# Attention and feed-forward block in one kernel: tile 1's load moved to SyncE's queue, tile 3's load behind a weight block, one transpose moved behind a pair's no-op

## Chip, cores and metric

One core of a Trainium2 chip. The metric is device time in microseconds (us); lower is better. Engines are named as in the profile: PE (TensorE, matmuls), DVE (VectorE), ACT (ScalarE), POOL (GpSimd), SP (SyncE, which here issues DMAs and carries no-ops).

## The reference

Two branches over the same normalized input are multiplied and added to the input. 2048 tokens, width 448, 16 heads of 28, feed-forward width 1792, bf16.

```
xn = layernorm(x)
q, k, v = split(xn @ wqkv)                 # 448 -> 3*448, 16 heads of 28
# each token attends to 8 tokens: itself and back in steps of 2
o = softmax(q . k[pos - 2*w] / sqrt(28), w = 0..7) . v
s = o @ wo                                 # 448 -> 448
g = silu(gelu(xn @ w1 + b1) @ w2 + b2)     # 448 -> 1792 -> 448
out = x + s * g
```

## The kernel before

The tokens are sorted into even and odd positions, so that the dilated window is a window of neighbours. They are cut into 16 token tiles of 128 rows and four chunks of four tiles. The stages are:

- **Normalization** of a token tile: statistics (line 354, BATCH_NORM_STATS2), their aggregate (358), root and reciprocal (366, 369), and the scaled tile `xn` (391 for tile 0, 422 for the others). The transposed form `xnT` of chunk 0 is made by PE transposes (404, 437) and copies (250, 252); from tile 4 on by a DMA transpose (301).
- **Projections** `qk_rows` (513) and `vproj` (536). The input width of 448 is three row tiles of 128 and a rest of 64, so the weights `w_in` are three loads, one for each row tile (`load_w`), and two tail loads.
- **Feed-forward** `ff1` (589) and its gelu (593), then `ff2_pair` and `ff2` (615, 641).
- **Attention** for nine blocks of tokens: `keys` (700, 698), `scores` (715), the exponentials (721), `values_sum` (746), the division (757, 762). Each block's rows go to a DRAM tile `o_rows` (769). `turn(t)` brings the rows of tiles t and t + 1 back transposed by one DMA transpose (301).
- **Output**: `final_pair` (780) and `final` (795) multiply by `wo`; `store` (803 to 815) gates, adds the input and writes out.

Every instruction group is a task of a plan. A table, ORDER, lists all tasks in the order in which they are emitted; the letter is the engine (P, V, A, G, S for PE, DVE, ACT, POOL, SP; D marks a DMA's landing, and emits nothing) and the number is the task. Each engine executes its own tasks in that order and waits by semaphores. A task's engine may be chosen by the letter where the task allows several.

Two things matter for this change. First, `pair` computes two jobs together on the two halves of PE's rows: a first half (f1), then a no-op on another engine that waits for the first half's last matmuls, then a second half (f3) that waits for the no-op:

```
def f2(k):
    held["told"] = {"POOL": nc.gpsimd, "SP": nc.sync, "ACT": nc.scalar}[k.on].nop()
    for i in held["last"]:
        behind(held["told"], i)
```

The engine of the no-op is the letter in ORDER. All that stands behind the no-op on that engine waits with it. Second, ahead of the first data PE runs idle matmuls on constants (line 265), ten of 512 columns and one of 128. The loads of the start are made by `load_x(t0, n, eng)` (tokens) and `load_w` (weights), all at line 288. The first matmuls on row tiles of tiles 0 and 1 are `first_batch`, in the order row tile 0, row tile 2, row tile 1, with three matmuls (q, k, v) for a token tile.

Of the kernel before, what the change touches and what calls it, by code (L numbers as in the profile page):

```python
# [11 lines left out]
ACT = mybir.ActivationFunctionType  # L12
# [2 lines left out]


ORDER = """
D0 A31 D32 G14 S29 D30 V12 P1 V13 V15 V19 V20 A48 V21 S33 D34 V22 V16 G45 V17 V18 P2 V23 G46 D47 S39 D40 P3 S35 D36
G95 P4 S37 D38 S41 D42 P5 S43 D44 P6 G97 P7 V55 P8 V56 S71 D72 V59 A57 P9 S73 D74 P10 G652 G24 S75 D76 G25 G28 G26 G27
S77 D78 V58 V99 P11 V60 P102 V100 A61 P103 V105 A106 A101 P128 V62 V109 V110 P111 P112 P132 P104 V113 A114 A107 D115  # L20
D108 P129 S81 D82 V63 P184 P133 V64 V67 A65 S83 D84 P130 V66 V116 P131 V117 V68 V185 P118 V98 A69 P119 V96 V120 D121
S85 D86 P134 V70 V122 P149 V123 A135 V136 A139 P124 G150 P125 A146 P151 A49 S137 D138 V126 D127 G147 D148 V142 P296
G140 D141 V152 P301 V153 G297 V91 S154 D155 P163 G302 V89 P298 V90 G164 V92 V87 G94 G264 G265 D266 P303 A300 V143 P165
V79 A305 S144 D145 P316 V194 A166 V198 A299 V195 G167 D168 P311 V199 S196 D197 V80 V88 V169 G317 G93 A304 P318 S200
D201 P306 A319 G312 V186 G170 D171 V187 V190 A320 G172 D173 P313 V191 S188 D189 G307 G174 D175 P156 V653 A314 G176
D177 V654 P308 A315 S192 D193 G157 G178 D179 P158 A310 P291 V159 A160 S256 D257 S258 D259 A309 P321 G292 S262 D263
G180 D181 S260 D261 P293 G322 G182 D183 P225 A294 P323 A295 G226 P227 A325 P267 P485 V229 A324 V273 S161 D162 P505
A228 G486 V275 V277 V279 P487 G506 V274 P495 A488 V276 V268 A489 P507 G496 V278 V280 P497 V282 A509 P475 V284 V286
A508 V283 V285 A498 P209 V288 G476 G210 V287 G281 A499 P477 V289 P216 V334 G217 G290 A478 V335 V338 S336 D337 P211
A479 V339 V330 P480 V213 S340 D341 V212 P218 V326 G481 P490 A219 V327 V331 S214 D215 A222 G220 D221 P482 G491 G223  # L30
D224 V683 P492 A484 S332 D333 V684 P500 A493 V412 A483 P202 V413 S328 D329 G501 A494 V400 P502 G203 V401 S402 D403
P204 A504 P655 V205 P580 A503 V206 S207 D208 S414 D415 A50 G248 D249 G250 D251 A656 P239 A658 A581 V657 V659 V408 V409
S410 D411 P582 G240 S230 D231 P660 V586 P685 A661 P241 V583 V404 V405 S406 D407 A663 P232 V245 V662 A686 P365 V713
V664 A688 G233 V714 A587 P234 A366 V687 V689 A242 P690 G923 V236 P367 A235 V588 P589 A691 S237 D238 G243 D244 A693
V692 V694 G246 D247 A584 S924 D925 A369 V585 S926 D927 A368 P715 S370 D371 G590 P695 P665 V696 A716 P591 V666 V697
A718 V667 V698 V668 V699 V669 G700 D701 P349 V592 G670 D671 S672 D673 P720 V595 A593 G350 P674 G702 D703 P351 V675
A721 G252 D253 V676 P416 A352 A353 G254 D255 A723 P342 G417 V677 S354 D355 V678 A596 P418 G343 V743 G679 D680 P704
V717 A420 P344 G681 D682 V705 A419 V706 P598 A346 S421 D422 V719 V707 A345 A744 V708 G709 D710 S347 D348 V597 G711
D712 P725 V722 G599 P745 V726 P750 V727 A746 P600 S928 D929 A748 V728 V729 A751 V724 G730 D731 S732 D733 A753 V594
V747 V749 P734 V604 P379 V735 A605 V736 P372 G380 V737 P381 V738 G373 P356 V601 G741 S739 D740 D742 A385 S930 D931  # L40
V773 A602 P755 G386 D387 P374 V756 G357 P358 A382 A375 V757 G383 D384 P430 A359 V774 A362 A376 P446 G360 D361 V758
V759 G363 D364 P775 S447 S760 D761 P448 G431 G762 D763 G388 D389 G392 D393 A776 V752 S377 D378 P780 A778 V449 P432
A781 V754 P423 S424 V803 A783 P764 V777 A450 P425 V765 A433 V766 P453 G390 D391 A436 V767 V768 P607 A427 A426 A804
A454 S769 D770 G394 D395 V779 G396 D397 G398 D399 V606 G434 D435 V603 G437 D438 P455 V782 G608 P439 V784 G771 D772
G271 D272 G269 D270 A459 V456 P805 G460 D461 V833 A440 P441 A806 G457 D458 P785 A808 P609 V786 A443 A442 A834 V787
V788 V789 G463 D464 G465 D466 S792 S428 D429 G790 D791 D793 V807 V809 S444 D445 G462 P810 V613 P540 A811 V610 A813
A541 P794 P815 V812 A51 G467 D468 P515 V795 V796 G469 D470 P542 V797 A516 V798 A611 P517 V816 G801 S799 D800 D802 V817
A544 P530 V818 A543 V819 P535 V814 A518 A531 G820 D821 V612 G822 D823 P824 A614 P532 A536 G471 D472 A519 V825 P537
V826 G473 D474 A534 P510 V827 V828 A539 V615 V863 P525 G829 D830 S831 D832 A533 A511 A538 P512 S526 A864 P520 P955
S521 S451 D452 A514 P527 G956 A513 P957 A528 P522 V958 A529 P944 V962 G959 A524 V963 P835 P840 A523 G945 S960 D961  # L50
P946 S964 D965 A52 P616 V947 V951 V952 A841 S953 D954 A843 V842 V948 A836 P865 V844 S949 D950 S934 D935 S932 D933 S936
D937 G617 P870 A838 V837 P618 A871 V839 A873 G872 A866 A868 V867 G874 A893 P845 V622 P625 G869 V846 V847 A623 V848
A894 V849 V619 G850 D851 V624 P854 G852 D853 A620 S626 P895 P627 V855 A896 V856 A898 V857 V858 V621 G859 D860 V897
G861 D862 V899 P550 V631 V628 P966 A632 G551 A629 V633 P900 G967 P977 A901 V630 A903 P968 V902 G978 A53 V904 P545 S938
D939 V973 P979 V974 G546 V969 S975 D976 P552 V980 G970 P905 A554 P547 V906 V907 S971 D972 A553 P555 V908 V981 A549
V909 S982 D983 P875 G556 P557 A548 V984 S910 D911 P884 S912 D913 V876 A559 P575 V877 A558 V885 P570 V886 S576 V887
V888 P577 S571 V878 G889 D890 P572 V879 A578 G891 D892 V985 P999 A579 G880 D881 S986 D987 P560 A574 G1000 G882 D883
A573 P1001 S561 P914 V1002 P562 V915 P565 V916 A563 V1003 A564 P988 V917 S566 S1004 D1005 V918 P567 S940 D941 V1006
G989 G921 P990 V1007 A568 P634 S1008 D1009 V995 A569 S919 D920 D922 V991 A54 V996 P635 V992 S997 D998 S993 D994 P638
V636 A637 S942 D943 P1015 P639 P1010 V640 P642 A641 V1011 V1012 V1016 S1013 D1014 P643 G1017 P646 S1018 D1019 V644  # L60
A645 P647 P1025 A648 P1020 V1026 V1027 P649 V1021 S1028 D1029 P650 P1030 V1022 A651 V1031 S1023 D1024 V1032 S1033
D1034
"""


# [58 lines left out]
def kernel(  # L124
# [13 lines left out]
    P = 128  # L138
# [17 lines left out]
    for v in range(9):  # L156
        n = NW - 1 if v == 4 else NW
# [10 lines left out]
    def rows(halves, pos, n):  # L168
        h, r = divmod(pos, HALF)
        return halves[h, r:r + n, :]  # L170
# [74 lines left out]
    def buf(pool, owner, i=0):  # L245
        return pool.bufs[owner.slots[pool][i]]
# [12 lines left out]

    t_on = plan.add("DMA", lambda _: None, ())  # L260
    t_warm = t_on
    for n in (512,) * 10 + (P,):
        def idle(k, n=n):
            one = nc.const_aps
            nc.tensor.matmul(buf(p_b, k)[:, :n], one.tensor(1.0, [P, P], BF16), one.tensor(1.0, [P, n], BF16), start=True, stop=True)
        t_warm = plan.add("PE", idle, [t_warm], take=(p_b,))
        t_warm.give = ((p_b, t_warm, 0),)
# [18 lines left out]
    def dma(eng, dst, src, deps=()):  # L286
        def fn(_):
            {"SP": nc.sync, "ACT": nc.scalar, "POOL": nc.gpsimd}[eng].dma_start(dst, src)  # L288
        a = plan.add(eng, fn, [t_on] + list(deps))
        return plan.add("DMA", lambda _: None, [a])  # L290
# [35 lines left out]
    load_w(2)  # L326
    tails = A_wqkv[KF:D, :].rearrange("p (w d) -> p w d", d=D)
# [649 lines left out]
```

## Time and profile before

| | |
|---|---|
| three runs | 148.98, 149.68, 151.68 us (median 149.68) |
| the profiled execution's own time | 149.42 us |
| its span, first to last instruction | 147.7 us |
| PE busy | 143.2 us (97%), 1827 matmuls |
| DVE, ACT, POOL busy | 104.7, 95.3, 56.7 us |
| HBM read and written | 9.70 and 6.29 MB |

Busy times are of one profiled execution; its time less its span, 149.42 - 147.7 = 1.7 us, lies outside the first and last instruction. Lines of the timeline give the start in us from the span's start, the duration, engine and line, what is written and read, the shape and the count, and in brackets the idle time ahead with what ended it. "SPq" is the issue of a DMA by SP, not its transfer. The ends of matmuls are modelled, their starts are recorded. Rows by stretches give busy time and count of PE, weight loads, DVE, ACT and POOL, then the granted clock, the share of the 16 DMA engines and GB/s.

### The profile page before, as it was taken

Reading aid. Unit: us, or ns where it says so; the run is one execution under the profiler, and the core shown is the slowest. Engines: PE = TensorE matmul, PEld = TensorE weight load, DVE = VectorE, ACT = ScalarE, POOL = GpSimd, SP = SyncE. Lnnn points to the kernel's source line nnn. Section 1 sums busy time; section 2 is a strip of 40 time slices with the busy share of each in tenths; the row PEclk is TensorE's granted clock in tenths of the full one; section 3 lists DMA queues with packets and bytes.
Section 4 is the critical chain, followed back from the end, with each engine's and each line's share of the span. In section 5 each row is a group of like instructions: output and inputs, shape, how many; then the busy total and the mean of one; then the engine's idle time right before and its main releaser. Section 6 shows DMA issues by size and latency. Waiting matters only on the chain.

```text
span 147.7 us, 4656 instructions
## 1 busy us (share of the span) xinstructions
PE 143.2 (97%) x1827; PEld 79.8 (54%) x1827; DVE 104.7 (71%) x290; ACT 95.3 (65%) x175; POOL 56.7 (38%) x113
## 2 busy tenths in 40 slices
PE   7999999999999999999999999999999999999991
PEld 2345555455566666666665554445565564545570
DVE  3879934179953798979969599728589996671642
ACT  4327576766684682785696889999983886571120
POOL 6743595105430031651476795512463024110200
PEclk9999999999999999999999999999999999999999
DMA  4999999999699799898499979993774332265112
GB/s 146 328 293 336 137 208 153 267 348 244 145 181 152 133 148 203 144 226 143 121 180 168 215 195 119 201 212 100 103 139 113 71 104 64 72 176 126 35 31 62
DMA packets 43966, 24.17 MB, mean 164 GB/s; under 512 B 33822, under 2 KB 42022, under 8 KB 43944
## 3 DMA queue, kind: packets, MB, share of 16 engines
q1 hardware_dynamic: 41080, 17.25, 62.4%
q0 software_dynamic: 2720, 6.51, 18.5%
q8 instruction: 14, 0.23, 0.7%
q10 hardware_dynamic: 144, 0.11, 0.3%
q14 instruction: 8, 0.07, 0.2%
HBM read 9.70 MB, written 6.29 MB: 108 GB/s over the span
## 4 chain that ended last, share of the span: by engine, by line
PE 90%; DMA 4%; DVE 1%; SPq 1%; issue 0%; DVEq 0%
PE bank L589 29%; PE bank L615 22%; PE bank L513 14%; PE bank L641 7%; PE bank L536 7%; PE bank L780 5%; DMA w_in<-in_A_wqkv_dram 4%; PE bank L746 3%; PE bank L715 3%; PE bank L795 1%; SPq L288 1%; DVE sg L803 1%; DVE o L811 0%; PE bank L437 0%; PE bank L898 0%
## 5 line engine op out<-in xcount | busy, mean ns | idle before, releaser
L589 PE MATMUL bank<-xnT,w 64*128 64x512 bf16 x392 | 46.6, 376 | 0.1
L593 ACT ACTIVATE h<-bank,b 128x512 bf16<-128x512 f32 x56 | 35.1, 685 | 13.4 <-PE bank L589 12.9
L615 PE MATMUL bank<-w,h 64*128 64x448 bf16 x336 | 33.8, 349 | 0.0
L589 PEld LDWEIGHTS <-w 64*128 64x128 bf16 x392 | 20.3, 94 | 19.1 <-issue 0.7
L513 PE MATMUL bank<-w_in,xnT 64*128 64x448 bf16 (+1 forms) x212 | 26.4, 350 | 0.2
L615 PEld LDWEIGHTS <-h 64*128 64x128 bf16 x336 | 17.3, 94 | 12.8
L762 DVE TENSOR_TENSOR a<-bank,rd 114x448 bf16<-114x448 f32 (+1 forms) x36 | 22.2, 622 | 1.1
L769 POOL DMA_DIRECT2D o_rows<-a x25 | 13.4, 538 | 24.8 <-DVE a L762 11.2
L721 ACT ACTIVATE E<-bank 128x456 bf16<-128x456 f32 (+1 forms) x36 | 17.4, 551 | 7.0 <-PE bank L715 5.9
L295 POOL DMA_DIRECT2D v<-v_rows x22 | 13.8, 633 | 9.9 <-PE bank L589 7.2
L513 PEld LDWEIGHTS <-xnT 64*128 64x128 bf16 (+1 forms) x212 | 11.2, 94 | 8.2 <-issue 0.6
L657 DVE TENSOR_TENSOR y<-bank,b 128x448 f32<-128x448 f32 x15 | 9.0, 621 | 8.2 <-PE bank L641 4.8
L295 POOL DMA_DIRECT2D v_rows<-v_tok x16 | 9.0, 566 | 14.3 <-PE bank L715 8.6
L536 PE MATMUL bank<-w_in,xnT 64*128 64x448 bf16 (+1 forms) x106 | 13.8, 349 | 0.0
L354 DVE BATCH_NORM_STATS2 st<-x_sb 128x6 f32<-128x448 bf16 x16 | 9.2, 609 | 4.5 <-DMA x_sb<-in_A_x_dram 4.5
L731 DVE TENSOR_TENSOR E<-E,m_gen 128x456 bf16<-128x456 bf16 (+1 forms) x29 | 10.8, 392 | 1.4 <-ACT E L721 1.3
L669 ACT ACTIVATE t<-y 128x448 f32<-128x448 f32 x12 | 6.9, 580 | 7.3 <-DVE y L657 7.3
L641 PE MATMUL bank<-w,h 128*128 128x448 bf16 (+2 forms) x70 | 11.4, 316 | 0.0
L700 DVE TENSOR_SCALAR kb<-qkT,plane 128x512 bf16<-128x512 bf16 x24 | 7.5, 358 | 3.5 <-DMA qkT<-qk_tok 2.1
L811 POOL TENSOR_TENSOR o<-x_sb,sg 128x448 bf16<-128x448 bf16 x3 | 3.1, 1031 | 16.7 <-DVE sg L803 8.7
L250 ACT CAST v_tok<-bank 128x448 bf16<-128x448 f32 x13 | 6.6, 534 | 4.3 <-issue 1.5
L757 DVE RECIPROCAL rd<-bank 114x8 f32<-114x8 f32 (+1 forms) x36 | 7.1, 199 | 2.6 <-PE bank L746 2.4
(86 smaller groups left out, 177.4 us busy)
## 6 DMA issues: line engine op xcount, KB each, us to landing
v_rows<-v_tok POOLq DMA_DIRECT2D x16, 128.0 KB, 3.9
v<-v_rows POOLq DMA_DIRECT2D x14, 128.0 KB, 4.7
out_dram<-o SPq DMA_DIRECT2D x15, 112.0 KB, 1.7
w<-in_B_w_dram SPq DMA_DIRECT2D x2, 784.0 KB
o_rows<-a POOLq DMA_DIRECT2D x23, 64.1 KB, 2.9
w<-in_B_w_dram SPq DMA_DIRECT2D x2, 672.0 KB
x_sb<-in_A_x_dram SPq DMA_DIRECT2D x3, 448.0 KB, 7.3
w_in<-in_A_wqkv_dram SPq DMA_DIRECT2D x3, 336.0 KB, 5.2
```

The costliest lines, as they stand in the source:

```text
L295: nc.gpsimd.dma_start(dst(k), src())
L354: nc.vector.bn_stats(out=buf(p_st, k)[:], in_=x_sb[:, t, :])
L513: return nc.tensor.matmul(ps[:, :D], xnT[r, kt, cs], w, start=start, stop=stop)
L536: return nc.tensor.matmul(ps[:, :D], xnT[r, kt, k0:k0 + P], w, start=start, stop=stop)
L589: return nc.tensor.matmul(ps[:], w1[r, kt, ms], xnT[r, kt, cs], start=start, stop=stop)
L593: nc.scalar.activation(buf(p_h, own, i)[:], buf(p_b, own, i)[:], ACT.Gelu_apprx_tanh, bias=b1[:, mt:mt + 1])
L615: return nc.tensor.matmul(ps[:, :D], buf(*h_at[(c, mt)])[r, j * P:(j + 1) * P], w2[r, mt, :], start=start, stop=stop)
L641: nc.tensor.matmul(ps[:, :n], buf(*h_at[(c, mt)])[:, j * P:(j + 1) * P], w2[:, mt, cs], start=(mt == 0 and not biased), stop=(mt == NMT - 1))
L721: nc.scalar.activation(buf(p_E, k)[:, :n], buf(p_b, a, r)[:, :n], ACT.Exp, scale=SCALE)
L731: (nc.gpsimd if k.on == "POOL" else nc.vector).tensor_tensor(out=E, in0=E, in1=m, op=ALU.mult)
L762: nc.vector.tensor_tensor(out=o, in0=sums(k, e)[:, :, :, :DH], in1=buf(p_rd, rd)[rows].unsqueeze(2).unsqueeze(3).to_broadcast((2 * nq, 8, ...
L769: (nc.gpsimd if k.on == "POOL" else nc.sync).dma_start(o_rows[n + i * nq:n + i * nq + nq, :], buf(p_a, own)[i * nq:i * nq + nq, i, :])
```

## The change

The code that makes tasks changes in two places. One idle matmul of 512 columns is left out, and the loads of tokens 1, 2 and 3 are three loads of one tile on SP, where there was one of tile 1 on ACT and one of tiles 2 and 3 on SP:

```diff
-    for n in (512,) * 10 + (P,):
+    for n in (512,) * 9 + (P,):
...
     load_x(0, 1, "SP")
-    load_x(1, 1, "ACT")
+    load_x(1, 1, "SP")
...
     load_w(0)
-    load_x(2, 2, "SP")
+    load_x(2, 1, "SP")
+    load_x(3, 1, "SP")
     load_w(1)
     load_w(2)
```

ORDER is renumbered throughout (lines behind the new load are one higher). Its tasks otherwise stand in their old order on each engine, but for the three places below. PE executes the same matmuls in the same order, less the idle one.

**SP at the start.** `x_sb` is the tokens, `w_in` 128x1344 a row tile of projection weights, `w_in` with 64 rows the tails. Before:

```order
L288 DMA x_sb<-in_A_x_dram 128x448
L288 DMA w_in<-in_A_wqkv_dram 128x1344 x2
L288 DMA x_sb<-in_A_x_dram 128x2x448
L288 DMA w_in<-in_A_wqkv_dram 128x1344
L288 DMA w_in_65<-in_A_wqkv_dram 64x2x448
L288 DMA w_in_65<-in_A_wqkv_dram 64x896
```

With the change:

```order
L288 DMA x_sb<-in_A_x_dram 128x448 x2
L288 DMA w_in<-in_A_wqkv_dram 128x1344 x2
L288 DMA x_sb<-in_A_x_dram 128x448
L288 DMA w_in<-in_A_wqkv_dram 128x1344
L288 DMA x_sb<-in_A_x_dram 128x448
L288 DMA w_in_65<-in_A_wqkv_dram 64x2x448
L288 DMA w_in_65<-in_A_wqkv_dram 64x896
```

Tile 1 is the second issue (before, it was ACT's first instruction). Then come row tiles 0 and 2, tile 2, row tile 1, tile 3 and the tails.

**DVE at the start**, from the statistics of tile 2 on. `st_96` and `st_97` are the statistics of tiles 2 and 3, `b_71` is the first bias, `m_first` and `m_gen` the attention masks. Before:

```order
L354 BN_STATS st_96<-x_sb 128x6
L358 BN_AGGR mv<-st_96 128x2
L354 BN_STATS st_97<-x_sb 128x6
L369 RECIPROCAL rstd<-sd 128x1
L422 TENSOR_SCALAR xn<-x_sb,mv,rstd 128x448
L427 COPY xn<-xn 128x64
L358 BN_AGGR mv<-st_97 128x2
L885 CAST b_71<-bank_155 128x14
L855 COPY m_first<-m_1_90 128x456
L855 COPY m_gen<-m_0_89 128x456
L252 COPY xnT<-bank_157 128x4x128
```

With the change:

```order
L355 BN_STATS st_96<-x_sb 128x6
L359 BN_AGGR mv<-st_96 128x2
L370 RECIPROCAL rstd<-sd 128x1
L423 TENSOR_SCALAR xn<-x_sb,mv,rstd 128x448
L428 COPY xn<-xn 128x64
L886 CAST b_71<-bank_154 128x14
L355 BN_STATS st_97<-x_sb 128x6
L359 BN_AGGR mv<-st_97 128x2
L252 COPY xnT<-bank_156 128x4x128
```

The statistics of tile 3 and their aggregate stand behind tile 2's normalization. The two mask copies are gone from this place; they follow the copy of tile 3's transposed form.

**SP in the middle.** `xnT<-o_rows` is `turn`, of tiles 0 and 1 in the first row and of tiles 2 and 3 in the second; `o_rows<-a` are stores of attention rows, `qkT` transposes of query and key tiles:

```order
 L301 DMA_TRANSPOSE xnT<-o_rows 128x4x256
-L769 DMA o_rows<-a 57x576 x2
+L770 DMA o_rows<-a 57x576 x3
+L301 DMA_TRANSPOSE qkT<-qk_tok_153 128x8x128
+L770 DMA o_rows<-a 57x576
 L301 DMA_TRANSPOSE xnT<-o_rows 128x4x256
-L769 DMA o_rows<-a 57x576
-L301 DMA_TRANSPOSE qkT<-qk_tok_153 128x8x128
-L769 DMA o_rows<-a 57x576
-L769 DMA o_rows<-a 56x576
+L770 DMA o_rows<-a 56x576
```

The transpose of tiles 2 and 3 stands three issues later. Directly ahead of it stands a no-op (not shown among the rows) that was ACT's: that of the pair which computes queries and keys of tile 14. In ORDER the place reads `A440 P441` before, and `S441 S931 D932 P442` with the change, where `S931` is the transpose.

More of the change, by code (lines that the diff above doesn't have):

```diff
@@ L23 @@
[L23 to L32, printed above, removed]
@@ L58 @@
[L58 to L62, printed above, removed]
+D0 G13 S28 D29 S30 D31 V11 P1 V12 V14 V18 V19 A49 V20 S32 D33 V21 V15 G46 V16 V17 P2 V22 G47 D48 S40 D41 P3 S34 D35
@@ L63 @@
+V1007 G990 G922 P991 V1008 A569 P635 S1009 D1010 V996 A570 S920 D921 D923 V992 A55 V997 P636 V993 S998 D999 S994 D995
+P639 V637 A638 S943 D944 P1016 P640 P1011 V641 P643 A642 V1012 V1013 V1017 S1014 D1015 P644 G1018 P647 S1019 D1020
+V645 A646 P648 P1026 A649 P1021 V1027 V1028 P650 V1022 S1029 D1030 P651 P1031 V1023 A652 V1032 S1024 D1025 V1033 S1034
+D1035
 """
```

70 lines of the change are left out of this document (40 added, 30 removed).

## Prediction

> **What bounds the kernel now.** I read the page's busy times first, then its chain, then the busy time by stretches, to see whether one engine sets the time everywhere.
>
> ```profile
> PE 143.2 (97%) x1827; PEld 79.8 (54%) x1827; DVE 104.7 (71%) x290; ACT 95.3 (65%) x175; POOL 56.7 (38%) x113
> PE 90%; DMA 4%; DVE 1%; SPq 1%; issue 0%; DVEq 0%
> core 0: us, PE busy (x) PEld busy (x) DVE busy (x) ACT busy (x) POOL busy (x), PEclk, DMA share, GB/s
> 5.30:10.50 5.20, 4.92 (x32) 2.53 (x32) 3.91 (x17) 2.04 (x7) 3.35 (x15) 1.00 1.05 327
> 40.00:100.00 60.00, 60.00 (x948) 35.73 (x946) 45.45 (x121) 44.91 (x86) 25.63 (x44) 1.00 1.01 170
> 100.00:144.40 44.40, 44.38 (x564) 24.47 (x558) 31.22 (x72) 26.85 (x47) 11.02 (x15) 1.00 0.39 94
> ```
>
> TensorE (PE) is busy for 60.00 of 60.00 us in the middle and 44.38 of 44.40 behind it. So no move there can bring time; it can only open a stall. What could be gained lies ahead of 10.50, where 5.20 us hold 4.92 of PE work, and the DMA part of the chain (4%) belongs there too. A gain of 2%, about 3.0 us, which is also about what a measurement of this kernel can tell from no change, has no room: the idle time of the whole span is 147.7 - 143.2 = 4.5 us, and most of it lies before the first matmul and behind the last.
>
> **The start: loads.** PE's rows, and the piece of the chain that ends there:
>
> ```profile
> 6.46 0.39 PE L437 MATMUL bank<-ident,xn 128*128 128x128 bf16 x4
> 6.99 0.54 PE L513 MATMUL bank<-w_in,xnT 128*128 128x448 bf16 x2
> 8.24 0.54 PE L513 MATMUL bank<-w_in,xnT 128*128 128x448 bf16 x2
> 8.61 0.35 PE L536 MATMUL bank<-w_in,xnT 128*128 128x448 bf16 x1
> 9.05 0.54 PE L513 MATMUL bank<-w_in,xnT 128*128 128x448 bf16 x2
> 2.66 6.35 DMA w_in<-in_A_wqkv_dram
> ```
>
> The batch at 9.05 waits for the third block of projection weights (row tile 1), issued at 2.66 and landed at 9.01. Matmuls of 448 columns start (8.61 - 8.24) / 2 = 0.19 us apart, so PE was ready at 8.61 + 0.19 = 8.80: 0.25 us of wait. The batch at 6.99 is the first one on row tile 2's weights; PE's work ahead of it ended at 6.46 + 0.39 = 6.85 by modelled ends, so 0.14 us more. No releaser is named for that gap; I take it for the load. These 0.39 us are all that better loads can give.
>
> ```profile
> 0.79 0.39 SPq L288 DMA_DIRECT2D x_sb<-in_A_x_dram  x1
> 1.25 0.89 SPq L288 DMA_DIRECT2D w_in<-in_A_wqkv_dram  x2
> 2.18 0.43 SPq L288 DMA_DIRECT2D x_sb<-in_A_x_dram  x1
> 2.66 1.88 SPq L288 DMA_DIRECT2D w_in<-in_A_wqkv_dram  x3
> DMA  5869999999967998999999999999999999999999
> DMA packets 1777, 2.59 MB, mean 316 GB/s; under 512 B 194, under 2 KB 1393, under 8 KB 1777
> 3.43 0.63 DVE L354 BATCH_NORM_STATS2 st<-x_sb 128x6 f32<-128x448 bf16 x1 [1.52 <-DMA x_sb<-in_A_x_dram]
> 4.19 0.59 DVE L354 BATCH_NORM_STATS2 st<-x_sb 128x6 f32<-128x448 bf16 x1
> 7.90 0.63 DVE L354 BATCH_NORM_STATS2 st<-x_sb 128x6 f32<-128x448 bf16 x1 [0.83 <-DMA x_sb<-in_A_x_dram]
> ```
>
> An issue on SP takes (2.66 - 0.79) / 4 = 0.47 us. Token tile 1, so far on ACT's queue, becomes SP's second issue, so both weight blocks are issued 0.47 us later. Is that the cost? The DMA row covers 1.8 to 10 us: the engines are full from about 2.4 on, at 316 GB/s. Then a landing is set by the bytes ahead. Row tile 2 has the same bytes ahead as before (tiles 0 and 1, row tile 0). Row tile 1 has one token tile (112 KB) fewer, since tile 3 moves behind it: 112 KB / 316 GB/s = 0.35 us earlier, of which PE can use the 0.25 it waited. Bounds: -0.39 (both waits go) to +0.47 (the issue decides). The DMA row is nearer to the byte reading; but the engines are not full in its first slices, so I take -0.15.
>
> The Trainium skill, "DMA: Bandwidth & Descriptors", section "Issuing engines are not separate DMA queues", says that SP and ACT each have only a ring on the same 16 engines. By that rule bringing tile 1 over to SP loses no bandwidth, and the whole price is the order; with separate engines per queue the load would cost SP's queue another 0.35 us. No row here separates the two.
>
> Tile 1 itself: tile 0 was issued at 0.79 and in use at 3.43, 2.64 later; tile 1, issued at 1.25, is then there at 3.89, and VectorE (DVE) reads it at 4.19. Hidden, with 0.30 to spare; the ScalarE issue that disappears is paid nowhere, as ACT then only loads a table.
>
> **The start: DVE.**
>
> ```profile
> 9.35 0.40 DVE L422 TENSOR_SCALAR xn<-x_sb,mv,rstd 128x448 bf16<-128x448 bf16 x1
> 10.02 0.27 DVE L855 COPY m_first<-m 128x456 bf16<-128x456 bf16 x1
> 10.61 0.42 DVE L252 COPY xnT<-bank 128x512 bf16<-128x512 bf16 x1
> 12.80 1.68 DVE L252 CAST qk_tok<-bank 128x448 bf16<-128x448 f32 x3
> 14.66 0.94 PE L536 MATMUL bank<-w_in,xnT 64*128 64x448 bf16 x8
> ```
>
> Tile 2's load is halved, so its statistics start about 0.35 before 7.90, and its normalization before 9.35. Tile 3 now lands behind row tile 1, at 8.66 + 0.35 = 9.0 by the same division, and its statistics (0.63) stand on DVE ahead of the copy at 10.61 that PE's next row pair needs. They end near 10.0, with the aggregate at 10.2: some 0.3 us to spare. If tile 3 came 0.5 late, that copy and PE behind it would be late by 0.2. The two mask copies (0.27 each) move behind tile 3, so the casts at 12.80 begin up to 0.54 later; the first ends near 13.9 instead of 13.4, and the first PE batch that takes one of their banks starts at 14.66. No cost; behind it 0.8 us are left.
>
> **The start: one idle matmul less.**
>
> ```profile
> 0.83 4.53 PE L265 MATMUL bank<-const-bfloat16-1.0 128*128 128x512 bf16 x11 [0.83 <-PEq L961]
> 5.28 0.73 PE L404 MATMUL bank<-ident,xn 128*128 128x128 bf16 x3
> PEclk9999999999999999999999999999999999999999
> ```
>
> Eleven idle matmuls (ten of 512 columns, one of 128: 10.25 units) take 4.53 us, 0.44 a unit; warm, 512 columns at the pace above would be 0.22. So PE runs at half pace there, though the granted-clock row prints full speed from its first slice: here the pace of the matmuls has to tell the clock. Dropping one ends them at about 4.9, and the transposes at 5.28 wait for DVE's data anyhow: no work is saved on the path. What it may cost is the clock: PE is idle for some 0.4 us just before pace doubles. If full pace came later, the four batches of three projection matmuls ahead of 9.05 would take 0.19 longer a matmul: 2.3, less the 0.39 of waits they fill, 1.9 us at most. Nothing is the lower end. I take 0, since 4.1 us of idle matmuls remain and the gap is a tenth of them.
>
> The Trainium skill, "TensorE: Matmul & The Clock Gate", Part 1, speaks against this edit: the gate opens after a busy window of about 3.4 us whose phase is free-running, so fewer phases now find a full window inside the idle matmuls. The trace agrees on the two paces, 0.44 and 0.22 us. A window missed whole, 3.4 us at half pace, would cost an estimated 1.7 us by that page; how much idling a window forgives no run here shows.
>
> **The middle: the no-op and the transpose.**
>
> ```profile
> 72.56 1.32 SPq L301 DMA_TRANSPOSE xnT<-o_rows  x1
> 75.51 0.25 SPq L769 DMA_DIRECT2D o_rows<-a  x1
> 79.70 0.24 SPq L769 DMA_DIRECT2D o_rows<-a  x1
> 82.42 0.92 PE L513 MATMUL bank<-w_in,xnT 64*128 64x448 bf16 x8
> 83.45 0.74 PE L513 MATMUL bank<-w_in,xnT 64*128 64x448 bf16 x6
> 86.19 0.32 SPq L769 DMA_DIRECT2D o_rows<-a  x1
> 97.06 0.35 PE L780 MATMUL bank<-wo,xnT 64*128 64x448 bf16 x1
> ```
>
> The pair of tile 14 has its first half at 82.42 and its second at 83.45; between them stands the no-op, now SP's. SP has nothing between 79.94 and 86.19, so the no-op is reached 3.4 us before the first half ends at 83.34, and passes on as ACT's did. Queued behind it: the transpose of tiles 2 and 3 (1.32, until about 84.7), then the row store of 86.19, untouched. Nothing was held up by the transpose at its old place either: SP's next issue, behind another pair's no-op, stands only at 75.51. The result, needed at 97.06, has 12.4 us from its new issue.
>
> ```profile
> 77.50:83.40 5.90, 5.90 (x92) 3.25 (x88) 4.83 (x14) 4.10 (x8) 4.12 (x8) 1.00 1.15 187
> 83.40:86.20 2.80, 2.80 (x56) 1.62 (x50) 2.02 (x7) 2.60 (x6) 2.63 (x5) 1.00 0.59 161
> 96.67 0.35 DVE L700 TENSOR_SCALAR kb<-qkT,plane 128x512 bf16<-128x512 bf16 x1 [1.35 <-DMA qkT<-qk_pair]
> 100.44 0.61 PE L715 MATMUL bank<-qkT,kb 64*128 64x57 bf16 x32
> ```
>
> The transpose's DMA work leaves a full stretch (share 1.15) for one at 0.59, where (1 - 0.59) x 2.80 = 1.15 us of all engines are free. I size it by its issue, 1.32; up to 0.2 us spill over to what follows. The tile that DVE awaits until 96.67 feeds the scores at 100.44, over 3 us later. Cost 0; at worst all 1.32 us go through ACT and DVE, which wait for that tile too, to PE.
>
> **Sum.** -0.15 (loads) + 0 (DVE) + 0 (idle matmul) + 0 (no-op, transpose), against the profiled execution's 149.42 us, its span of 147.7 and 1.7 around it: 149.27, so **149.3 us**. That execution lies 0.26 below the median of the three, 149.68.
>
> **Rivals.**
> - *Loads gain all.* Both weight blocks land before PE asks: 149.42 - 0.39 = 149.0. For it: 0.35 us fewer bytes ahead of row tile 1. Against: row tile 2 has no fewer. Chance 0.13.
> - *Slower: the clock opens late.* Place: 5.3 to 9 us; price up to 1.9: 149.42 + 1.9 = 151.3, half of it 150.4. It decides once the idle time of 4.9 to 5.28 keeps the gate shut. Against: PE idles a little even now and gets its pace. For: the three runs before span 2.7 us, so something already differs between executions. Chance 0.12.
> - *Slower: the middle stalls.* The no-op is reached late, because SP is held by the row store at 79.70, or the moved transpose pushes the tile of 96.67. The first costs PE nothing until that store is 3.4 us late, then one for one; the second 1.32 at most: 150.7. Chance 0.10.
> - *Nothing moves*, since SP's extra issue eats what fewer bytes give: 149.4, not to be told from the forecast, and counted with it.
>
> **How the numbers follow.** The forecast with its neighbour has 0.65: 149.3, its own range 148.6 to 150.2. With the rivals the range is 148.4 to 151.2; the low end allows for the spread of single runs (148.98 to 151.68), the high end takes in most of the late clock and the middle's stall. Faster by over 2% would need more idle time than PE has: 0.03. Slower by over 2% needs 3 us: a store over 6 us late, or the late clock and the stall together, or something unseen: 0.10. Within 2%: 0.87.
>
> **What would show it.** Right: PE's batch at 9.05 starts at 8.8 to 9.05, tile 3's statistics stand on DVE between 9 and 10 us ahead of the 10.61 copy, the second half of tile 14's pair starts within 0.1 us of the first half's end, and PE's busy share from 40 to 144 stays whole. Wrong: projection matmuls 0.38 us apart behind 6 us (clock); row tile 1 landing at 9.3 or later (issue decides); a PE gap near 83.4 (no-op) or 100 (transpose).

## The result, and the profile after

| | before | changed |
|---|---|---|
| median of 21 runs each | 149.67 us (148.64 to 151.68) | 150.12 us (148.93 to 151.85) |
| ratio, 95% interval | 1 | 1.0049 (1.0026 to 1.0072) |
| profiled execution, its span | 149.42, 147.7 us | 150.32, 148.6 us |

The change costs 0.49%. That is within 2%, and the time lies in the predicted range, but the sign is wrong: the forecast was slightly faster, and the interval (1.0026 to 1.0072) excludes a kernel that is as fast as the one before. Ratios here and below compare fast executions alone while medians take in all, so a ratio is not the quotient of two medians, and the profiles of e3 and e9 are of slow executions (151.80 and 152.30 us) and stand outside the table below.

Busy times of the page and two stretches (columns as in the prediction's rows):

```profile
PE 143.1 (96%) x1826; PEld 79.2 (53%) x1826; DVE 105.2 (71%) x290; ACT 95.0 (64%) x175; POOL 56.9 (38%) x113
40.00:100.00 60.00, 60.00 (x948) 35.63 (x944) 45.77 (x124) 44.30 (x85) 26.59 (x46) 1.00 0.97 173
100.00:145.40 45.40, 45.35 (x572) 24.94 (x568) 31.94 (x73) 27.85 (x49) 11.03 (x15) 1.00 0.39 93
```

From 40 us on PE is as full as before. So the 0.9 us of longer span arose earlier. PE's timeline of the changed kernel, from the first transposes to chunk 1's first `ff1` pair:

```profile
4.75 0.64 PE L405 MATMUL bank<-ident,xn 128*128 128x128 bf16 x3
6.18 0.54 PE L514 MATMUL bank<-w_in,xnT 128*128 128x448 bf16 x2
8.00 0.54 PE L514 MATMUL bank<-w_in,xnT 128*128 128x448 bf16 x2
10.04 0.93 PE L514 MATMUL bank<-w_in,xnT 64*128 64x448 bf16 x8
12.46 1.03 PE L590 MATMUL bank<-xnT,w 64*128 64x512 bf16 x7 [0.49 <-DMA w<-in_B_w_dram]
26.07 0.91 PE L514 MATMUL bank<-w_in,xnT 64*128 64x448 bf16 x7 [0.40 <-DVE qk_pair L252]
28.95 2.33 PE L590 MATMUL bank<-xnT,w 64*128 64x512 bf16 x20 [0.46 <-DMA xnT<-xn]
```

and the last of these places before:

```profile
11.09 0.93 PE L513 MATMUL bank<-w_in,xnT 64*128 64x448 bf16 x8
12.94 0.61 PE L589 MATMUL bank<-xnT,w 64*128 64x512 bf16 x4
28.05 2.32 PE L589 MATMUL bank<-xnT,w 64*128 64x512 bf16 x19
```

The start did gain: the row pair of tiles 2 and 3 starts 1.05 us earlier (10.04 for 11.09), the first `ff1` pair still 0.48. About half of that gain is tile 0, which is there 0.58 us earlier now that tile 1's load follows it on SP. DVE's first statistics show it (3.43 before):

```profile
2.85 0.63 DVE L355 BATCH_NORM_STATS2 st<-x_sb 128x6 f32<-128x448 bf16 x1 [0.94 <-DMA x_sb<-in_A_x_dram]
```

They start at 2.84 to 2.94 in all eleven profiles of kernels that load tile 1 from SP, and at 3.33 to 3.51 in the nine that load it from ACT.

Behind the start PE waits three times, as the brackets of its rows show: for w1's first half at 12.46, for a bank that DVE frees at 26.07, for chunk 1's transposed rows at 28.95. At this last place it is 0.90 us late, and this 0.90 arrives at the end of the span (148.6 - 147.7).

What is late shows on SP and DVE. SP's transposes of both kernels, the changed one first:

```profile
11.31 9.29 SPq L301 DMA_TRANSPOSE qkT<-qk_tok  x3
20.70 5.27 SPq L301 DMA_TRANSPOSE xnT<-xn  x4
```

```profile
12.36 7.52 SPq L301 DMA_TRANSPOSE qkT<-qk_tok  x3
19.97 5.16 SPq L301 DMA_TRANSPOSE xnT<-xn  x4
```

The three query/key transposes start 1.05 earlier and are through 0.72 later (20.60 for 19.88). Chunk 1's rows, `xnT<-xn`, stand behind them in SP's queue and are issued by 25.97 instead of 25.13, 0.84 later. DVE of the changed kernel, and the first of these rows before:

```profile
14.34 1.16 DVE L355 BATCH_NORM_STATS2 st<-x_sb 128x6 f32<-128x448 bf16 x2 [0.53 <-DMA x_sb<-in_A_x_dram]
24.30 1.18 DVE L701 TENSOR_SCALAR kb<-qkT,plane 128x512 bf16<-128x512 bf16 x4 [3.12 <-DMA qkT<-qk_tok]
25.41 0.60 DVE L252 CAST qk_pair<-bank 128x448 bf16<-128x448 f32 x1
```

```profile
23.38 1.15 DVE L700 TENSOR_SCALAR kb<-qkT,plane 128x512 bf16<-128x512 bf16 x4 [2.15 <-DMA qkT<-qk_tok]
```

DVE's key copies wait 3.12 us for the third transpose, and the cast that frees PE's bank stands behind them. DVE also waited 0.53 for tiles 4 to 7. So the loads behind the start are late, though no byte was added to them. Two things could make them late. They are issued later, since SP has two loads more ahead of them: w1's first half at 5.51 instead of 4.58, tiles 4 to 7 at 7.32 instead of 6.97. And fewer bytes move at the start. The transfers between 3 and 4 us, changed and before (last column GB/s):

```profile
3.00:4.00 1.00, 1.00 (x4) 0.37 (x3) 0.97 (x3) 0.21 (x1) 0.81 (x4) 1.00 0.81 159
```

```profile
3.00:4.00 1.00, 1.00 (x4) 0.36 (x3) 0.57 (x1) 0.00 (x0) 0.81 (x4) 1.00 1.19 328
```

With tiles 0 and 1 one behind the other on one queue and the first weight block third, half the bytes move in that microsecond. This holds for all profiles: 137 to 237 GB/s in the ten with tile 1 as SP's second issue, 279 to 364 in the nine with it on ACT. Over the first 20 us it is 225 to 241 GB/s against 235 to 254, the same direction with overlap.

**A measure for the rest.** From the row pair (10.04, 11.09) to chunk 1's first `ff1` pair PE has the same work in all kernels. The smallest distance is 16.80 us, and ten profiles have it within 0.01. What lies over 16.80 is waiting (in the changed kernel 2.11 us, of which the three rows above name 1.35). A kernel whose row pair comes late can show 0.00 because its data had more time, so the two columns ahead are to be read with it:

| kernel | row pair | chunk 1 | over 16.80 |
|---|---|---|---|
| before | 11.09 | 28.05 | 0.16 |
| changed; again (e16); third (e18) | 10.04; 10.53; 10.45 | 28.95; 28.45; 29.28 | 2.11; 1.12; 2.03 |
| e1 start alone | 10.35 | 27.85 | 0.70 |
| e12 tile 1 on SP alone | 10.38 | 27.57 | 0.39 |
| e5 w1's second half on ACT | 10.41 | 28.42 | 1.21 |
| e13 three waits opened | 10.55 | 27.58 | 0.23 |
| e2, e4, e6, e8, e10, e14, e15, e17 (tile 1 on ACT) | 10.44 to 11.54 | 27.25 to 28.34 | 0.00 |
| e7 tails on ACT; e11 weights second | 12.69; 11.11 | 29.49; 27.91 | 0.00 |

The profiles of e3 (tile 1 on SP alone, as e12) and e9 would stand at 2.91 and 0.51.

### The profile page after: what moved, and what is told of

Same layout as the page of the kernel before. It is cut to its first block, busy times and chain, and to the rows that moved or that the text cites. A ratio compares the mean times of both kernels' runs of the same rounds, so it can differ in the third digit from the quotient of the medians.

```text
span 148.6 us, 4654 instructions
## 1 busy us (share of the span) xinstructions
PE 143.1 (96%) x1826; PEld 79.2 (53%) x1826; DVE 105.2 (71%) x290; ACT 95.0 (64%) x175; POOL 56.9 (38%) x113
## 4 chain that ended last, share of the span: by engine, by line
PE 77%; DMA 12%; SPq 4%; DVE 3%; issue 1%; DVEq 0%
PE bank L590 22%; PE bank L616 21%; PE bank L514 10%; PE bank L642 7%; PE bank L537 5%; PE bank L781 5%; DMA x_sb<-in_A_x_dram 5%; DMA qkT<-qk_tok 5%; SPq L288 4%; DMA xnT<-xn 3%; PE bank L747 3%; PE bank L716 3%; PE bank L796 1%; DVE st L355 1%; DVE sg L804 1%
## 5 line engine op out<-in xcount | busy, mean ns | idle before, releaser
L590 PE MATMUL bank<-xnT,w 64*128 64x512 bf16 x392 | 47.9, 376 | 0.9 <-DMA w<-in_B_w_dram 0.5
L514 PE MATMUL bank<-w_in,xnT 64*128 64x448 bf16 (+1 forms) x212 | 27.2, 350 | 0.4 <-DVE qk_pair L252 0.4
L537 PE MATMUL bank<-w_in,xnT 64*128 64x448 bf16 (+1 forms) x106 | 14.2, 349 | 0.0
```

Of the source, the lines that this page charges most:

```text
L514: return nc.tensor.matmul(ps[:, :D], xnT[r, kt, cs], w, start=start, stop=stop)
L537: return nc.tensor.matmul(ps[:, :D], xnT[r, kt, k0:k0 + P], w, start=start, stop=stop)
L590: return nc.tensor.matmul(ps[:], w1[r, kt, ms], xnT[r, kt, cs], start=start, stop=stop)
```

## The experiments

All ratios are to the kernel before, on the same chip; each kernel has 12 times, e16 has 6.

### e1, e2: which half of the change

The theory ("A" in the expectations): the loss is chunk 1's rows, turned late. The rivals: the middle, chance, or one edit of the start by itself. e1 is the changed kernel with the middle of before; e2 the kernel before with the middle of the change (its ORDER has the task numbers of the kernel before):

```diff
 e1
-A386 V774 A603 P756
+A386 S931 D932 V774 A603 P756
...
-V834 S441 S931 D932 P442
+V834 A441 P442
 e2
-A385 S930 D931 V773 A602
+A385 V773 A602
...
-V833 A440 P441
+V833 S440 S930 D931 P441
```

> All edits of the start as in the change (token tile 1 on SP's queue, tiles 2 and 3 loaded apart, statistics reordered, one idle matmul less); the middle as before. Theory A (the start's loads put the first query/key transposes ahead of the same loads of w1 and tiles 4 to 7, these transposes then finish later, and tile 4 to 7's normalised rows turn later): the whole loss is here, 1.005 of the time before (about +0.7 us), first transposes near 4.75 us, chunk 1's first ff1 pair near 28.9 us instead of 28.05. Theory E (the no-op and the transposes in the middle cost it): no loss, 0.997 to 1.001. Theory F (the late transposes are chance of one execution): 1.000 on the median.

> Only the middle of the change: the no-op on SP, two output transposes behind it; the start as before. Theory A: 1.000 (within 0.001), since the two profiles stand 0.97 to 0.99 us apart on both sides of the edit. Theory E: 1.005.

Measured: e1 150.05 us, 1.0035 (1.0000 to 1.0070); e2 149.08 us, 0.9988 (0.9960 to 1.0016). The two intervals overlap a little, but e1 has PE wait 0.70 at chunk 1 and e2 nowhere: the loss sits in the start. The rows of e2 show more: its start is that of before, and yet its transposes are through at 18.46, where the profile of before had 19.88.

```profile
10.49 0.93 PE L513 MATMUL bank<-w_in,xnT 64*128 64x448 bf16 x8
11.76 6.70 SPq L301 DMA_TRANSPOSE qkT<-qk_tok  x3
27.29 2.98 PE L589 MATMUL bank<-xnT,w 64*128 64x512 bf16 x26
```

The same steps in the same order ended up to 1.4 us apart between executions. So 0.60 of the 1.05 us that the start seemed to gain was a late execution of before. The four profiles with the start of before have the row pair at 10.49 (e2), 10.54 (e14), 11.09 and 11.54 (e6, where PE waits 0.87 for the second weight block), the seven with the whole new start at 10.04 to 10.55.

### e3, e12, e4: one edit of the start at a time

e3 and e12 are one kernel, before with tile 1 on SP; e4 is before with tiles 2 and 3 apart and DVE's new order:

```diff
 e3, e12
-    load_x(1, 1, "ACT")
+    load_x(1, 1, "SP")
 e4
-    load_x(2, 2, "SP")
+    load_x(2, 1, "SP")
+    load_x(3, 1, "SP")
```

> Only token tile 1's load moved from ACT's queue to SP's, second there. Theory A: tile 0 lands near 2.8 us instead of 3.41 and the first transposes start near 4.8 us; whether the loss comes with it tells whether the earlier first rows alone do the harm: 1.002 to 1.005 if they do. Theory B (the queue that tile 1 takes costs it, because each SP load then stands behind one more): the same 1.005 with w1 and tiles 4 to 7 landing over 0.3 us later than before. If split loads matter instead: 1.000.

> Only tile 1's load on SP's queue, the rest as before: the kernel of e3 again, whose interval (0.997 to 1.004) left open whether this edit alone costs anything. Theory G: 1.002 to 1.005 over both sets of runs. If tile 1's queue only costs together with the split of tiles 2 and 3: 1.000.

> Only tiles 2 and 3 loaded apart (tile 3 behind row tile 1) and the vector engine's order of the start that goes with it; tile 1 on ACT's queue and ten idle matmuls as before. Theory A: row tile 1 lands near 7.6 to 8.0 us, so the first rows gain 0.5 to 1.0 us at 8 us; the qkT transposes go out earlier and the loss is here: 1.003 to 1.005. Theory C (one more DMA and the later copies of masks cost it): the same, but with the gap at the first ff1 batch or at a mask, not at 25 to 29 us. If tile 1's queue is the cause: 1.000.

Measured: e3 149.58 us, 1.0006 (0.9968 to 1.0044); e12 149.68, 1.0002 (0.9964 to 1.0040); e4 149.50, 1.0006 (0.9967 to 1.0045). Neither edit alone has a cost that these runs show; the 1.002 to 1.005 that was expected of e12 isn't met, though its interval doesn't exclude it. The profiles say more about tile 1: e12's has 0.39 us of waits and e4's none, and e3's, of one of that kernel's longest executions, has PE wait 1.00 at 26.81 and 0.81 at 30.05. Both profiles of this kernel have the thin transfers too (184 and 175 GB/s between 3 and 4 us).

### e5, e6: is it SP's own queue?

The first form of theory A said that the transposes stand behind w1's second half in SP's queue. These kernels issue it from ACT, the changed kernel (e5) and the one before (e6):

```diff
+        q = "ACT" if i else "SP"
-        t_w1.append([dma("SP", w1[:, 0:3, cs], ktiles(B_w1[0:KF, cs]))]
-                    + [dma("SP", w1[64 * i:64 * i + 64, 3, cs], B_w1[KF:D, cs]) for i in range(2)])
+        t_w1.append([dma(q, w1[:, 0:3, cs], ktiles(B_w1[0:KF, cs]))]
+                    + [dma(q, w1[64 * h:64 * h + 64, 3, cs], B_w1[KF:D, cs]) for h in range(2)])
```

> The changed kernel with the three loads of w1's second half issued from ACT's queue, behind tile 2's deviation, instead of SP's; the first query/key transposes on SP then stand behind no load of w1's second half in their own queue. Theory A (the lost gain is these transposes behind that backlog): the three transposes are through SP's queue 1 us or more before 20.6 us, the first ff1 pair of chunk 1 starts near 28.1 to 28.5 us instead of 28.95, and the time is 148.7 to 149.6, under the changed kernel's 150.1. Rival (the engines are simply full with bytes, whichever queue they come from): transposes still end near 20 us, 150.0. Rival F (chance): the ratio to the kernel before stays between 1.000 and 1.007.

> The kernel before with the same move of w1's second half to ACT's queue. Theory A: its own transposes end earlier too, but its tensor engine, which starts later, has little left to wait for at 25 to 29 us, so 0.995 to 1.000; the scatter of its runs (148.6 to 151.3) shrinks. Rival (bytes): 1.000.

Measured: e5 149.94 us, 1.0041 (1.0003 to 1.0078); e6 149.55, 1.0003 (0.9971 to 1.0035). e5's issues on ACT and SP's transposes:

```profile
7.70 1.63 ACTq L288 DMA_DIRECT2D w<-in_B_w_dram  x3
11.68 7.96 SPq L301 DMA_TRANSPOSE qkT<-qk_tok  x3
```

The transposes are through at 19.64, for 20.06 to 20.63 in the changed kernel's three profiles (and 19.41 in e1), and the time stays. The test isn't clean, since the edit does two things. SP is held less by the three issues (1.33, 2.39 and 1.45 us, for 1.95, 3.40 and 3.29 in the changed kernel), and PE no longer waits at 26 and 28 us. But w1's second half now moves together with tiles 4 to 7. These, issued at 7.32 in both kernels, are there at 15.69 instead of 14.34; what the third transpose reads comes later by as much, and PE waits at 18.21 and 19.55 instead (0.27 and 0.29). So e5 moves the loss and doesn't settle what SP's queue order is worth. The Trainium skill, "DMA: Bandwidth & Descriptors", section "Issuing engines are not separate DMA queues", says that transfers started by different engines run on the same 16 DMA engines and interleave. The trace agrees (15.69 for 14.34).

### e7, e8, e11: what makes the loads late

e7 issues the two tail loads of the changed kernel from ACT, e8 puts tile 1 back on ACT and leaves all else of the change, e11 issues the first weight block ahead of tile 1:

```diff
 e7
-dma("SP", w_in3[:64], ...), dma("SP", w_in3[64:], ...)
+dma("ACT", w_in3[:64], ...), dma("ACT", w_in3[64:], ...)
 e8
-    load_x(1, 1, "SP")
+    load_x(1, 1, "ACT")
 e11
-D0 G13 S28 D29 S30 D31 V11 P1 V12 V14 V18 V19 A49 V20 S32 D33
+D0 G13 S28 D29 V11 P1 V12 V14 V18 V19 A49 V20 S32 D33 S30 D31
```

> The changed kernel with the two loads of the weights' last rows (the tails of w_in) issued from ACT's queue behind the first deviation, so that SP issues two loads less ahead of w1 and tiles 4 to 7. Theory G (the loss is SP's issue time: each load costs its queue about 0.46 us, and the change puts two more there, so w1 and tiles 4 to 7 land 0.8 us later): tiles 4 to 7 land near 13.4 us instead of 14.3, w1's second half near 16.9 instead of 17.8, and the time falls to 148.9 to 149.6. Theory A without G (only that the transposes are issued earlier): 150.0 as the changed kernel.

> The changed kernel with token tile 1 back on ACT's queue: tiles 2 and 3 apart, one idle matmul less and the middle's no-op stay. Theory G with the hole (with tiles 0 and 1 on one queue the transfers between 3 and 4 us fall from 328 to 159 GB/s, which is never made up): the hole is filled again, 149.2 to 149.7, a ratio to before of 0.997 to 1.001. If the split of tiles 2 and 3 alone does it: 1.003 to 1.005.

> The changed kernel with the first weight load ahead of tile 1's on SP, so that the transfers between 3 and 4 us aren't thin; SP issues as many loads as in the changed kernel. Theory G by bytes (the loads are late because 0.17 MB were not moved at 3 to 4 us): over 280 GB/s there, tiles 4 to 7 land 0.3 to 0.8 us earlier, first ff1 pair 0.3 to 0.6 us later since tile 1 comes later, chunk 1 no later: 149.2 to 149.7. Theory G by issues (each issue on SP's queue counts): tiles 4 to 7 as late as in the changed kernel, and the tile that comes later adds: 150.0 to 150.5.

Measured: e7 149.66 us, 1.0039 (0.9998 to 1.0081); e8 149.14, 0.9973 (0.9939 to 1.0007); e11 150.43, 1.0069 (1.0032 to 1.0106). e8, its transfers between 3 and 4 us and its rows:

```profile
3.00:4.00 1.00, 1.00 (x4) 0.36 (x3) 0.61 (x1) 0.00 (x0) 0.81 (x4) 1.00 1.00 352
10.44 0.93 PE L514 MATMUL bank<-w_in,xnT 64*128 64x448 bf16 x8
11.85 7.50 SPq L301 DMA_TRANSPOSE qkT<-qk_tok  x3
27.25 2.98 PE L590 MATMUL bank<-xnT,w 64*128 64x512 bf16 x26
```

With tile 1 on ACT the rate is 352 GB/s again, the transposes are through at 19.35, chunk 1 starts without a wait, and the loss is gone. This is the edit that carries it. It doesn't tell bytes from issues, since SP's later loads are issued 0.49 us earlier too. e11 was to tell them apart: as many issues on SP as the changed kernel, but the large block second.

```profile
3.00:4.00 1.00, 1.00 (x4) 0.36 (x3) 0.71 (x2) 0.16 (x1) 0.81 (x4) 1.00 0.98 351
```

The rate is back. w1 and tiles 4 to 7 are issued when the changed kernel issues them (5.51 and 7.32), and yet the third transpose lands earlier: DVE's key copies start at 22.67, for 23.68 to 24.30 in the changed kernel's three profiles (23.00 in e1). This speaks for the bytes. The time does not: 150.43 is what was expected if issues count, and the 149.2 to 149.7 expected of the bytes failed. Tile 1 came later, and PE's first transposes with it (5.90 for 4.75), which also helps to make the waits vanish. In this profile chunk 1 starts at 27.91, as early as before, and 0.64 us are lost behind it, 0.40 of them near 100 us, with no wait named. What costs e11 its time is open.

e7 shows no wait at chunk 1 for another reason: PE is late itself. Its tails went ahead of the projection weights, and PE waited at once:

```profile
6.23 0.91 PE L514 MATMUL bank<-w_in,xnT 128*128 128x448 bf16 x2 [0.72 <-DMA w_in<-in_A_wqkv_dram]
7.73 0.95 PE L514 MATMUL bank<-w_in,xnT 128*128 128x448 bf16 x2
```

Behind that wait the projection matmuls start 0.35 to 0.38 us apart, half the pace of the changed kernel's first profile (0.19), until about 9.9 us, while the granted-clock column prints 1.00. From 6.23 to the pair at 10.08 PE needs 3.85 us; the same work takes the changed kernel 2.06 (5.37 to 7.43). So 1.79 us go with the pace, in this execution of 150.82 us. How many of e7's other runs have it isn't known.

### e9, e10: opening the waits, first try

Chunk 1's row transposes ahead of the third query/key transpose on SP, the key copies behind the two query/key casts on DVE; e9 on the changed kernel, e10 with tile 1 on ACT as well. The instructions that move, as runs of the engine's order:

```diff
 SP
-qkT<-qk_tok x3, xnT<-xn x4
+qkT<-qk_tok x2, xnT<-xn x4, qkT<-qk_tok
 DVE
-kb<-qkT,plane x4, CAST qk_pair, CAST qk_tok
+CAST qk_pair, CAST qk_tok, kb<-qkT,plane x4
```

> The changed kernel with the four transposes of chunk 1's normalised rows put ahead of the third query/key transpose in SP's queue, and the vector engine's four key copies that need that transpose put behind the two query/key casts. Loads and start are those of the changed kernel. Theory A (the loss is a stall of 0.5 to 1 us at 25 to 29 us, because these rows turn late): no wait of the tensor engine between 24 and 30 us, the first ff1 pair of chunk 1 within 15.9 us of the first of chunk 0 (17.35 in the changed kernel's profile), 148.6 to 149.4, a ratio of 0.995 to 1.000. Rival (something else of the start costs it, and the stall only shows there): 1.003 to 1.005.

> The same, with token tile 1 on ACT's queue as before the change: the start's gain without the late loads, and the rows of chunk 1 ahead. If both parts of the theory hold this is the fastest: 148.4 to 149.0, 0.993 to 0.998, and few runs over 149.5.

Measured: e9 150.69 us, 1.0058 (1.0019 to 1.0096); e10 150.31, 1.0024 (0.9982 to 1.0066): slower than expected. In e10's profile chunk 1 starts without a wait, at 27.54, but a new one stands 6 us on (in e9's too, 1.76 us at 34.98). PE, and DVE ahead of it:

```profile
33.95 0.93 PE L514 MATMUL bank<-w_in,xnT 64*128 64x448 bf16 x8 [0.84 <-DVE b L901]
```

```profile
31.04 2.21 DVE L355 BATCH_NORM_STATS2 st<-x_sb 128x6 f32<-128x448 bf16 x4 [2.02 <-DMA x_sb<-in_A_x_dram]
33.31 0.59 DVE L901 CAST b<-bank 128x448 bf16<-128x448 f32 x1
```

The cast of the second bias frees the bank that PE needs, and stands behind chunk 2's statistics, which wait for tiles 8 to 11. The wait had moved to another place.

### e13 to e16: all three waits opened

The six statistics rows ahead of that cast move behind it, on top of the orders of e9. The three waits meant here are those for chunk 1's rows, for the bank whose cast stands behind DVE's key copies, and for the bank whose bias cast stands behind chunk 2's statistics; the one for w1's first half is left as it was. e13 is the changed kernel so, e14 the one before, e15 the changed one with tile 1 on ACT; e16 is the changed kernel as it is.

```diff
 DVE
-BN_STATS st x4, BN_AGGR mv x2, CAST b
+CAST b, BN_STATS st x4, BN_AGGR mv x2
```

> The changed kernel with three waits opened: chunk 1's rows turn ahead of the third query/key transpose, the key copies stand behind the query/key casts, and the cast of b2 stands ahead of chunk 2's statistics. Theory A (the loss is these waits): no wait of the tensor engine over 0.2 us from the first ff1 pair to 40 us, 148.6 to 149.3 us, and at least 0.4% under the changed kernel of the same call (e16). Rival (the loss sits before 12.5 us or elsewhere): within 0.2% of e16.

> The kernel before with the same three waits opened. Theory A: its median is made of runs in which these waits cost nothing (about half, near 148.8) and runs in which loads land late (149.7 to 150.3); the latter lose part of their excess: 148.7 to 149.3, ratio 0.995 to 0.999. Rival: 1.000, if late runs lose their time before 12.5 us.

> The changed kernel with tile 1 on ACT's queue and the three waits opened. Theory A: 148.4 to 149.0, ratio 0.993 to 0.998; equal to or under e13. If tile 1 on SP brings an earlier start that only these waits ate, e13 is the faster of the two by 0.1 to 0.3 us.

> The changed kernel as it is, a second profile and times beside e13 to e15. Theory A: over 0.5 us of waits of the tensor engine between 24 and 34 us again, 1.003 to 1.006. If the waits of the first profile were chance, this profile has none and the ratio still stands near 1.005.

| | median (range), us | ratio, 95% interval |
|---|---|---|
| e13 changed, opened | 148.90 (148.23 to 150.36) | 0.9976 (0.9936 to 1.0017) |
| e14 before, opened | 148.88 (148.69 to 149.65) | 0.9972 (0.9937 to 1.0006) |
| e15 tile 1 on ACT, opened | 148.71 (148.64 to 148.84) | 0.9959 (0.9931 to 0.9987) |
| e16 changed | 151.19 (150.34 to 152.27) | 1.0115 (1.0058 to 1.0173) |

Chunk 1's first `ff1` pair in e13, in e15, and in e16:

```profile
27.58 2.77 PE L590 MATMUL bank<-xnT,w 64*128 64x512 bf16 x24
```

```profile
27.54 2.77 PE L590 MATMUL bank<-xnT,w 64*128 64x512 bf16 x24
```

```profile
28.45 1.90 PE L590 MATMUL bank<-xnT,w 64*128 64x512 bf16 x16 [0.61 <-DMA xnT<-xn]
101.56 0.35 PE L781 MATMUL bank<-wo,xnT 64*128 64x448 bf16 x1 [1.33 <-ACT h L594]
```

With the waits opened the changed kernel loses nothing: e13 and e14 are equal, and e13 lies 2.29 us under e16 on the same chip, from a row pair at the same time (10.55 and 10.53). e15 beats both kernels, and its twelve times lie within 0.20 us, where those of before on that chip lie within 2.18; e13's still spread over 2.13. The reorders on the kernel before alone (e14) show a gain of 0.28% that their interval doesn't separate from none. e16 is worse than the first comparison, and its profile has a second stall at 101.56, so not all of the 2.29 is the three waits.

### e17, e18: a share of the middle?

e17 is e15 with the middle of before, e18 the changed kernel a third time.

```diff
 e17
-A386 V774 A603 P756
+A386 S931 D932 V774 A603 P756
...
-V834 S441 S931 D932 P442
+V834 A441 P442
```

> As e15 (tile 1 on ACT, the three waits opened), with the middle as before the change. Theory A: 148.6 to 148.9 us and 0.994 to 0.998 as e15, so that the middle edit is worth nothing either way. If the middle edit costs (its transpose ahead of tile 14's): under e15's ratio by 0.2% or more, 0.992 to 0.994.

> The changed kernel a third time. Theory A: 0.5 us or more of waits between 24 and 34 us in its profile, a ratio of 1.003 to 1.007, and at 100 us a stall only by chance (0 to 2 us). If the middle edit makes the stall at 100 us, it shows here too, over 0.5 us.

Measured: e17 149.11 us, 0.9987 (0.9952 to 1.0023); e18 150.28, 1.0052 (1.0018 to 1.0087), which repeats the first comparison. e18's profile has no wait of PE between 80 and 120 us, and at chunk 1:

```profile
29.28 1.04 PE L590 MATMUL bank<-xnT,w 64*128 64x512 bf16 x8 [0.86 <-DMA xnT<-xn]
```

So the stall at 101 us doesn't come with every execution of the change. From the first matmul of `final` to the scores behind the next `ff2` PE needs 7.04 us in sixteen of the twenty profiles, but 9.48 in e16, 8.37 in e9, 7.44 in e11 and 7.33 in e3. The first three of these have the moved transpose, as nine of the sixteen have; e3 has the old place. The stall stands where the prediction's rival of the middle looked for it: ahead of it ACT waits 3.2 us for transposed query and key tiles. Whether the moved transpose favours it is open.

e17's expectation failed by a little: it isn't as fast as e15, and at 148.46 to 150.93 it scatters as e15 did not. Its profile has a wait that e15's has not, 0.79 us at 79.53 for ACT, behind a DMA. Of all profiles only e1's has one at this place too (0.22), and both kernels have the old middle. Its interval overlaps e15's, so e15's lead on e17, and with it a gain from the moved transpose, isn't settled.

## Why the prediction failed

- **PE as the bound, and where there is room.** Right from 40 us on, as the two stretches show. But the prediction took the full PE of the middle as proof for all behind 10.50, and shows no row of 10.5 to 40. "It can only open a stall" was the right sentence; the stall came just there, and no term of the sum stood for it. In that stretch PE is busy for 28.16 of 29.50 us in the changed kernel, and before for 29.41:

```profile
10.50:40.00 29.50, 29.41 (x283) 15.62 (x283) 20.64 (x64) 19.62 (x34) 12.94 (x22) 1.00 1.14 232
```

- **The loads at the start** is the step that failed, in what it counted. The term of -0.15 follows the bytes up to row tile 1, for PE's first batches, and stops. Behind row tile 1 in the same queue stand w1's first half, tiles 4 to 7, w1's second half and the transposes. The missing term is the wait up to chunk 1: 1.12 to 2.11 us over 16.80 in the three profiles of the change, 0.00 to 0.16 in the four with the start of before. For the row pair itself the sign of -0.15 was right; its size can't be read from starts that spread over 1 us (10.49 to 11.54, 10.04 to 10.55).
- **Tile 0** was put at nothing. The prediction followed tile 1 and held that the first transposes wait for DVE's data anyhow; tile 0 came 0.58 us earlier, and these transposes started at 4.75 instead of 5.28. So the gain was larger than forecast at the first batches and was lost behind them.
- **Bytes or issues.** The prediction decided for bytes and held the engines full from about 2.4 us on; it did not ask whether the new order keeps them full. Two loads of 112 KB issued 0.47 us apart do not: 112 KB / 0.47 us is 244 GB/s at most, an estimate from the issue times, and 137 to 237 were measured. So the sentence that moving tile 1 to SP "loses no bandwidth" did not come true here. The bound of +0.47, "the issue decides", was priced for PE's first batches only.
- **The bounds** (-0.39 to +0.47) rested on one execution, in which both later weight blocks were late. In e2, with the same start, the batch on row tile 2 follows the transposes ahead by 0.23 us (6.41 to 6.64). So the wait there was 6.99 - 6.46 - 0.23 = 0.30 us and not the 0.14 that modelled ends gave, and "all that better loads can give" was too small by that much.
- **DVE's order, tile 1's 0.30 to spare:** hidden as forecast in the first profile, where DVE reads tile 1 at 3.61; in e18 it waits for it until 4.12. Tile 3's statistics stood ahead of the copy that PE needs, and no wait of PE names them. The rival that loads gain all looked at the right place, the start, and expected the wrong direction.
- **The idle matmul:** no cost in the first profile. The two projection matmuls at 6.18 and at 8.00 take 0.54 us as a pair, as in the first batches of before. But the rival of the late clock isn't out: with nine idle matmuls the first batch of e13 and e16 runs at half pace (0.93 us for its first pair) until about 6.5 us and their row pair starts 0.5 later than in the first profile, and in e7 half pace lasts to about 9.9 and costs 1.79, near the 1.9 that the prediction gave as the most. With ten idle matmuls the slowest first pair is e4's (0.81). No run leaves out the idle matmul alone, so what it costs on the median isn't known, and the full pace of the first profile was in part luck.
- **The middle:** right in the first profile, and e2 shows no cost on the median. The pair of tile 14 in the changed kernel, and the moved transpose:

```profile
83.41 0.92 PE L514 MATMUL bank<-w_in,xnT 64*128 64x448 bf16 x8
84.43 0.74 PE L514 MATMUL bank<-w_in,xnT 64*128 64x448 bf16 x6
```

```profile
84.58 1.24 SPq L301 DMA_TRANSPOSE xnT<-o_rows  x1
```

The second half starts 0.10 us behind the first half's end (83.41 + 0.92 = 84.33), the transpose is through at 85.82, before SP's next row store. The rival's stall near 100 us stands in e16's profile all the same, where that place takes 2.44 us longer (9.48 for 7.04).

What is shown: the loss is in the start (e1, e2), goes when tile 1 is back on ACT (e8), and goes when the three waits are opened (e13 beside e16, e13 equal to e14). That the thin transfers between 3 and 4 us are the link is argued and not shown: e8 changes the issues as well, e11 has the rate and the early landings back but not the time, and e3 and e12 have thin transfers without a cost that can be measured. So it stays open why tile 1's move alone costs nothing measurable (the runs allow up to 0.4%) while e8 lies nearly 0.8% under the whole change (0.9973 against 1.0049, from different sets of runs).

## What to carry to other kernels

When a load is moved, follow the queue past the first consumer: name what stands behind it, to the last load before the engines run empty, and who waits for each landing. A start that is earlier by a few tenths is worth nothing if the next stage's data have a fixed time of arrival. Where such a wait can't be made shorter, put what doesn't need the late data ahead of it on every in-order engine: here three such reorders on SP and DVE took the whole loss of the change away (e13). The same reorders with tile 1 on ACT gave 0.4% under the kernel before in one set of runs (e15); with the old middle (e17) that gain wasn't there.

## What the runs showed of the hardware

- The same steps end up to 1.4 us apart from one execution to the next (query/key transposes through at 18.46 in e2, 19.88 in the profile of before, with the same start; PE starts on the second weight block at 6.64 in e2 and waits for it until 7.63 in e6). A difference of that size at one place of two profiles says nothing yet; the medians and a repeat do.
- With two loads of 112 KB at the head of SP's queue, issued 0.47 us apart, 137 to 237 GB/s moved between 3 and 4 us (ten profiles); with the second of them on ACT's queue, 279 to 364 (nine).
- The issue of a DMA transpose held SP for 1.22 to 1.34 us in the four of chunk 1's rows, and for 1.95, 3.40 and 3.29 us in the three query/key transposes ahead of them, while w1 and tiles 4 to 7 were on their way (1.33, 2.39 and 2.89 before). What sets the difference isn't shown.
- PE's pace doubles at different times from one execution to the next: at about 6.5 us in e16 and 9.9 in e7, where the granted-clock column prints 1.00 all along, and ahead of the first projections (5.37) in the changed kernel's first profile.
